# A new order for the first 430 entries of a hand-listed schedule, with new engines and PSUM pairs

## The chip, the cores and the metric

The kernel runs on one core of a Trainium2 chip. The metric is the device time of one execution in microseconds (us); lower is better. In this text PE is the matmul engine (TensorE), DVE, ACT and POOL are VectorE, ScalarE and GpSimd, and SP is the engine that issues the DMAs.

## The reference

A linear recurrence over 768 time steps (4 batches, 8 heads, head dimension 40), and behind it a two-layer MLP (320 to 2048 to 320) on its 3072 output rows, all in FP32:

```python
for t in range(S):
    y[:, :, t] = einsum('bhd,bhde->bhe', rt, state)
    Sa = einsum('bhde,bhe->bhd', state, at)
    state = state * wt[:, :, None, :] - einsum('bhd,bhe->bhde', Sa, bt) + einsum('bhd,bhe->bhde', vt, kt)
x = y.transpose(0, 2, 1, 3).reshape(B * S, H * D)
h = x @ w_in
out = (h / (1 + exp(-1.702 * h))) @ w_out
```

## The kernel before

Time is cut into 12 chunks of 64 steps, and the batches into two pairs: 24 units, numbered i = 2 x chunk + pair. Within a unit the recurrence is written as small matrices of one head and one chunk (64x64), four of which share the array as 64x64 quadrants. For each unit there are these steps, by the names of their PSUM tiles:

- `ps_cum` and `ps_cumc`: running sums of the logarithm of the decay, by time and by channel. ACT makes the factors FT, GT, wch (from `ps_cumc`) and G (from `ps_cum`) of them; products with FT and GT scale the inputs `ak` and `b` in place, products with G make `kh` and `bh`.
- `ps_A`, `ps_RV`, `ps_N`: scores. `ps_N` needs the scaled `ak` and `b` and begins the inversion of a triangular matrix; `ps_A` and `ps_RV` are masked by DVE into A and RV.
- `ps_level`: five rounds of that inversion. Each round is a matmul task (with an `ident` part in units 0 to 3), a copy of PSUM to PT or W, and a transposition into EX by DVE, on which the next round waits. Then `ps_Q` and `ps_T` finish the matrix T.
- `ps_B` (two halves), `ps_X`: the right side and the solution M; for chunks behind the first also `ps_zT` and `ps_rz`, which read the state.
- `ps_y`: the output and the new state. Units of one pair follow each other through the state, so unit 2 needs unit 0's `ps_y`, and unit 3 unit 1's.

The output of two units goes to memory and comes back turned as `xT_all`, and the chunk's MLP follows: `ps_up` (40 tasks a chunk, 64x256 matmuls), the gelu on ACT into g, and `ps_down`. The weights arrive as FP64 in eight pieces of four DMAs each (`w_sb`, `extra` and `xT_all` hold the raw pieces) and are turned into FP32 by ACT, DVE and POOL (L447 to L463).

Nothing sets the order but a list. Every step is a task with its possible engines, and `ORDER` names all 2700 tasks in the order in which they are issued: an entry is the task's number, a letter for the engine (p PE, a ACT, d DVE, g POOL, s SP) and, for tasks that use PSUM, which of four PSUM pairs they take. `Plan.listed` reads it:

```python
for one in text.split():
    e = next(e for e in ENGINES if ENGINES[e] in one)
    n, bank = one.split(ENGINES[e])
    t = self.tasks[int(n)]
    assert e in t.engines and t.after <= done and (e == "SP" or (t.pair is None) == (not bank))
    t.engine, t.bank = e, int(bank or 0)
```

and the kernel ends in `for t in plan.listed(ORDER): t.fn(t)`. Each engine works off its entries in the order of the list; between engines semaphores hold a task back until what it needs is there. All DMAs are issued by SP in one queue. Matmuls all stand in one helper, `mm`, which is line L300 of the profile.

Numbers that help to follow the list, for unit 0: 87 `ps_cum`, 88 `ps_cumc`, 89 and 90 the factors, 93 to 95 the products, 98 `ps_A`, 100 `ps_RV`, 103 `ps_N`, 107, 110, 113, 116 and 119 the five levels, 126 `ps_Q`, 128 `ps_T`, 130 and 132 `ps_B`, 134 `ps_X`, 136 `ps_y`. Unit 1: 142, 143 sums, 154 A, 156 RV, 159 N, 163 to 175 the levels, 190 X, 192 y. Unit 2: 264, 265 sums, 288 N, 292 to 304 the levels, 316 zT, 319 rz, 321 and 323 B. Unit 3: 334, 335 sums, 353 A, 355 RV, 358 N, 362 to 374 the levels, 386 zT, 389 rz. 198 to 207, 209 to 218 and so on are `ps_up`. DMAs of unit 0: 0 logw, 5 ak (two DMAs), 6 b (two), 7 rv (two), 8 RV, 9 time.

Of the kernel before, what the change touches and what calls it, by code (L numbers as in the profile page):

```python
# [119 lines left out]
214p1 389p2 66d 472a3 483g 204p0 390a2 560s 371p3 67d 306a 53s 215p1 71s 482s 216p1 372a3 217p1 476a 220p2 373d3 68g 218p1  # L120
221p2 477d 219a1 205p0 222p2 206p0 223p2 224p2 207p0 55a 311p3 225p2 79s 312d3 80s 226p2 208a0 58d 313p1 374p3 314d1 227p2 56d
379a3 228p2 229p2 57d 326p0 230a2 59g 393p1 327d0 378a3 391p2 394a1 375d3 231p0 558s 392d2 376a 232p0 233p0 395d1 559s 81s 73a
78s 234p0 480s 381p2 235p0 328p1 481s 382a2 74d 377a3 485d 380a3 236p0 75d 492a 242p2 486d 243p2 82a 76d 484d 77g 383p3 237p0
384d3 244p2 329d1 330d1 488p3 473d 238p0 531d 245p2 487g 246p2 489d3 85d 532p1 239p0 533a1 396p3 331d 332s 474s 475s 534a1
240p0 247p2 397d3 562s 241a0 535p1 83d 490p3 536a1 84d 398p0 572a 491d3 86g 550p1 555s 561s 253p3 399d0 551a 333s 400d0 254p3
401d 402s 554s 255p3 552a1 564d 493p0 705s 556a 567g 570p1 403s 494d0 248p2 563d 566g 249p2 495d0 498d 256p3 571d1 565g 250a2
496a0 251d2 252s 696p1 497g 557d 539p0 537p2 704s 257p3 538a2 540d0 258p3 553d 611d 697a 499d 573p2 784s 700s 259p3 576a2
574d2 710d 260p3 541d0 575d2 404p0 578d 261a3 577g 405p0 579d 698a1 568p2 711g 500p1 406p0 569d2 501a1 407p0 262d3 263s 708s
580p2 702a 502d1 408p0 582d2 409p0 503d 410p0 583d 504a 612p3 411p0 584g 613d3 412p0 614d3 413p0 505p1 709d 414a0 426p3 506d1
427p3 428p3 507d1 429p3 699d 581d2 430p3 615p1 785s 706s 701s 703d 431p3 616a1 585p0 432p3 508d 586a0 433p3 587d0 434p3 509a  # L130
588d 435p3 589d 448p2 436a3 510p1 590p0 511a1 449p2 592d0 591a0 512d1 415p3 513d 416p3 593d 514a 417p3 594g 418p3 515p0 419p3
# [4 lines left out]
623d0 780s 776a 549s 756d 730p3 624p0 456d2 457d2 731d3 458s 459p2 777a1 778g 732d3 786s 788g 781a 779s 626d0 460p2 625d0 627g
733d 795p1 835d 734a 461p2 735p3 791g 462p2 628s 736a3 796d1 737d3 716p0 792g 738d 463p2 782d 739g 1011s 920p1 757p3 925s
464p2 717d0 758a3 629s 759a3 790d 465p2 740p0 789d 466p2 741a0 742d0 921a 797p3 467d2 760p0 1008s 468d2 800a3 923d 652p2 469s
761d0 922a1 653p2 926a 930s 798d3 714p1 799d3 654p2 924s 802d 801g 655p2 934d 803a 656p2 836p0 657p2 715d1 658p2 659p2 837d0
762p3 838d0 927d 660p2 763a3 661p2 764p1 662a2 743d 630p0 744d 928s 631p0 632p0 765d1 804p3 766d1 633p0 805a3 806d3 634p0 807d  # L140
635p0 808a 745p2 636p0 748d2 637p0 749d2 839p1 933g 750d2 638p0 840a1 1009s 751d2 639p0 809p3 746d2 935g 640a0 641p1 810d3
642p1 793p2 747a 811d3 674p0 812d 794d2 813a 752p3 643p1 753a3 814p2 644p1 815a2 816d2 754p3 645p1 755d3 646p1 817d 647p1 818a
767p2 841p3 768d2 648p1 842a3 649p1 819p2 650p1 820a2 821d2 675p0 769p3 822d 651a1 823d 771d3 931s 770d3 772g 824p2 936d 676p0
827a2 828a2 942p1 829a2 677p0 1153s 830a2 937d 945a1 773s 663p3 825d2 664p3 943d1 1156s 826a 665p3 944d1 999p2 947d 946g 666p3
1000a 1004s 980d 940p1 948g 667p3 941d1 668p3 774s 669p3 670p3 831p1 671p3 1001a2 1002d 1003s 832d1 672p3 1005a 1013d 678p0
673a3 1006d 833p2 843p1 679p0 834d2 1007s 844d1 938p2 845d1 680p0 939d2 846p3 681p0 847d3 949p1 1012g 682d0 848p2 950a1 683d0
1014d 684s 685p3 849d2 1015g 1010s 850d2 1021p0 1016g 951d1 686p3 1024a0 1232s 851d 1235s 981p2 687p3 982a2 952d 852s 1022d0
983a2 953g 1144p1 1023d0 688p3 1026d 1145a 1149s 1025d 1027g 984p2 1059d 689p3 1154s 954p0 853s 985a2 1147g 690p3 1158d 1148s
955a0 956d0 986p2 1146a1 957d 1150a 691p3 958d 987a2 1151d 988p0 692p3 989a0 1152s 990d0 959p1 693a3 865p2 960a1 694d3 866p2
961d1 867p2 695s 962d 868p2 963d 1028p0 869p2 1029a0 1030d0 870p2 1031d 1157g 871p2 1159d 1032a 1060p3 872p2 873p2 1061a3  # L150
874p2 1062d3 1033p1 875a2 854p0 1035d1 855p0 1036d 856p0 1037d 1063p3 857p0 1064d3 1034a1 858p0 964p2 859p0 965a2 966d2 1038p1
967d 860p0 1039a1 1040d1 861p0 1041d 1017p3 968a 1042g 862p0 1018d3 863p0 969p2 864a0 876p1 970d2 877p1 972d2 971g 1043p3
973d2 878p1 1044a3 974d2 879p1 975d2 880p1 881p1 1045d3 1019p0 1046d 976p2 1047a 882p1 1020d0 1233s 883p1 977a2 1166p3 884p1
1169a3 1167d3 1377s 978p0 885p1 1168d3 898p2 1171d 1170g 886a1 979d0 887p3 1172a 1048p0 991p1 1051a0 888p3 1052a0 992d1 889p3
1053a0 890p3 1054a0 891p3 1049d0 993p1 1050a 1067p0 994d1 1160g 1155s 892p3 1161d 1068a0 893p3 894p3 1069d0 1380s 895p3 1204d
1065p0 995d1 896p3 996d 1066a0 1231s 1055p1 899p2 897a3 1056d1 997s 1173p0 1223p3 900p2 1174a0 1175d0 1228s 1176d 1224a 1177g
1057p1 901p2 1058d1 1070p0 998s 1164p1 1225a3 1226d 1236g 1227s 1071d0 902p2 1229a 1165d1 1162p3 903p2 1238d 1163d3 904p2
1237d 1178p0 1230d 905p2 1179a0 1180d0 1245p1 906a2 1181d 1072p3 1248a1 1456s 907d2 1182g 1246d1 908s 1247d1 909p0 1250d 1234s
1239g 1073d3 1251a 910p0 1240g 1074d3 1249d 1183p2 1459s 1283d 1368p1 911p0 1184a2 1075d 1373s 912p0 1185d2 1369a 1076s 1186d
# [978 lines left out]
```

## Time and profile before

| | |
|---|---|
| device time, three runs | 678.22, 678.64, 679.32 us (median 678.64) |
| span of the profiled execution | 676.5 us; no separate time is given for it, so the runs' median stands beside it, 2.1 us above |
| PE busy | 648.5 us, 96% of the span |
| DVE, ACT, POOL busy | 444.6, 331.6, 175.3 us |
| DMA | 69.74 MB, mean 103 GB/s |

The profile counts times from the first instruction. In the views, "<-" behind an idle time names what ended it; "issue" is a wait with no semaphore that the profile shows. A matmul of the program stands as two in the trace (FP32 takes two passes), so 16 matmuls of a task are "x32". The granted clock is 1.00 at full speed and 0.50 at half.

### The profile page before, as it was taken

What the parts mean: (1) busy time and instruction counts of PE and PEld (TensorE: products, weight loads), DVE (VectorE), ACT (ScalarE), POOL (GpSimd) and SP (SyncE); (2) the same over time, 40 slices, a digit from 0 to 9 for tenths busy, and PEclk for the clock granted to TensorE, in tenths of its full rate; (3) what the DMA queues carried; (4) which work ended last, traced back from release to release, by engine and by line L of the source; (5) the groups of instructions that cost most, each with busy time, mean ns of one, the idle gap of its engine ahead of it and who ended that gap; (6) DMA issues with size and microseconds to landing.
All of it is one profiled execution on the core that took longest, in us unless ns stands there. A gap on an engine that the chain in (4) does not pass through costs nothing.

```text
span 676.5 us, 42217 instructions
## 1 busy us (share of the span) xinstructions
PE 648.5 (96%) x19488; PEld 553.4 (82%) x19488; DVE 444.6 (66%) x908; ACT 331.6 (49%) x710; POOL 175.3 (26%) x204
## 2 busy tenths in 40 slices
PE   5768999999999999999999999999999999999997
PEld 5657887987998987788888888798888798798785
DVE  4786787777867667767776587768656766675001
ACT  4676755534564655664545445455454354252110
POOL 6344244224123123123123211322412421300000
PEclk9899999999999999999999999999999999999999
DMA  7983736315314314432404413513412411200200
GB/s 230 300 289 94 232 107 187 103 43 154 108 47 149 93 58 117 121 108 72 118 22 132 141 34 109 156 33 108 140 39 71 122 53 54 61 14 15 61 12 20
DMA packets 35313, 69.74 MB, mean 103 GB/s; under 512 B 5440, under 2 KB 14656, under 8 KB 35136
## 3 DMA queue, kind: packets, MB, share of 16 engines
q1 hardware_dynamic: 35136, 67.03, 32.6%
q8 instruction: 153, 2.51, 1.5%
q14 instruction: 24, 0.20, 0.1%
HBM read 59.15 MB, written 7.86 MB: 99 GB/s over the span
## 4 chain that ended last, share of the span: by engine, by line
PE 93%; DMA 2%; DVE 2%; issue 1%; ACT 1%; DVEq 0%; SPq 0%; ACTq 0%
PE ps_up L300 31%; PE ps_down L300 30%; PE ps_level L300 9%; PE ps_y L300 5%; PE ps_B L300 5%; PE ps_X L300 2%; PE ps_N L300 2%; PE ps_rz L300 2%; PE ps_RV L300 2%; PE ps_A L300 2%; PE ps_zT L300 1%; DMA ak<-in_ak 1%; PE ps_cum L300 1%; PE ps_T L300 1%; DMA b<-in_b 1%
## 5 line engine op out<-in xcount | busy, mean ns | idle before, releaser
L300 PE MATMUL ps_up<-xT_all,w_sb 64*64 64x256 f32 x3840 | 251.0, 377 | 0.8 <-issue 0.4
L300 PE MATMUL ps_down<-w_sb,g 64*64 64x320 f32 x3072 | 237.0, 430 | 0.2 <-ACT zr L877 0.2
L300 PEld LDWEIGHTS ps_up<-xT_all,w_sb 64*64 64x64 f32 x3840 | 170.1, 133 | 15.9 <-issue 1.5
L300 PEld LDWEIGHTS ps_down<-w_sb,g 64*64 64x64 f32 x3072 | 128.0, 133 | 42.8 <-ACT zr L877 0.4
L996 ACT ACTIVATE g<-ps_up 128x1024 f32<-128x1024 f32 x48 | 49.2, 1024 | 45.4 <-PE ps_up L300 45.0
L715 POOL TENSOR_TENSOR EX<-ES,quads 128x512 f32<-128x512 f32 x29 | 38.3, 1322 | 112.7 <-DVE ES L708 74.9
L300 PEld LDWEIGHTS ps_level<-W,EX 64*64 64x64 f32 x2560 | 57.8, 134 | 6.7 <-DVE T L838 0.5
L758 ACT COPY W<-ps_level 128x512 f32<-128x512 f32 (+1 forms) x56 | 29.5, 527 | 67.7 <-PE ps_level L300 65.7
L760 DVE TENSOR_TENSOR E<-two,ps_level 128x256 f32<-128x256 f32 x80 | 33.1, 415 | 34.2 <-ACT W L758 30.1
L300 PE MATMUL ps_level<-W,EX 64*64 64x64 f32 (+1 forms) x2560 | 55.4, 217 | 0.1
L713 ACT ACTIVATE EX<-ES,quads 128x256 f32<-128x256 f32 x80 | 36.3, 501 | 31.0 <-DVE ES L708 30.3
L619 POOL TENSOR_TENSOR ak<-ak,FT 128x512 f32<-128x512 f32 x16 | 20.9, 1305 | 76.6 <-DMA ak<-in_ak 53.4
L708 DVE STREAM_TRANSPOSE ES<-E 128x256 f32<-128x256 f32 x80 | 35.3, 443 | 4.4
L300 PE MATMUL ps_level<-PT,EX 64*64 64x64 f32 (+2 forms) x1280 | 32.8, 235 | 5.1 <-DVE EX L729 3.7
L300 PEld LDWEIGHTS ps_level<-PT,EX 64*64 64x64 f32 x1280 | 30.8, 139 | 8.3 <-DVE EX L729 4.2
L300 PE MATMUL ps_y<-M,bh 64*64 64x104 f32 (+1 forms) x768 | 35.6, 250 | 0.7 <-DVE M L915 0.4
L300 PE MATMUL ps_y<-RV,kh 64*64 64x104 f32 (+1 forms) x768 | 35.6, 251 | 0.0
L899 ACT COPY B<-ps_B 128x416 f32<-128x416 f32 (+1 forms) x34 | 16.6, 492 | 33.4 <-PE ps_B L300 33.2
L300 PEld LDWEIGHTS ps_y<-RV,kh 64*64 64x64 f32 x768 | 28.3, 137 | 2.6 <-DVE M L915 0.5
L689 DVE COPY_PREDICATED PT<-within,ps_N 128x256 f32<-128x256 uint32 x40 | 17.8, 444 | 18.5 <-ACT P L697 13.5
L915 DVE TENSOR_TENSOR M<-ps_X,later 128x832 f32<-128x832 f32 (+1 forms) x24 | 23.8, 993 | 8.3 <-PE ps_X L300 8.1
L300 PE MATMUL ps_B<-RV,A 64*64 64x104 f32 (+1 forms) x768 | 27.9, 252 | 1.1 <-issue 1.1
(131 smaller groups left out, 1088.2 us busy)
## 6 DMA issues: line engine op xcount, KB each, us to landing
ak<-in_ak SPq DMA_DIRECT2D x48, 160.0 KB
rv<-in_rv SPq DMA_DIRECT2D x48, 160.0 KB
time<-in_time SPq DMA_DIRECT2D x24, 320.0 KB
xT_all<-x_dram SPq DMA_DIRECT2D x48, 160.0 KB
wc<-in_wc SPq DMA_DIRECT2D x20, 264.0 KB
logw<-in_w SPq DMA_DIRECT2D x24, 160.0 KB
...
```

Of the source, the lines that this page charges most:

```text
L300: nc.tensor.matmul(o, lhsT, rhs, start=start, stop=True, skip_group_check=True)
L619: plan.add(R, {"DVE": 690.0, "POOL": 1270.0, "sbuf": True}, lambda t: of(t.engine).tensor_mul(ahT(), ahT(), FT_of(i)), reads=T("ak", "FT") ...
L689: plan.add(R, dve(256), lambda t, n=n: nc.vector.copy_predicated(tiles_of(at(E0_t, i)), every(within_of(n), [128, 2, 4, 32]), blocks(psum( ...
L708: plan.add(rank, dve(256), lambda t: nc.vector.transpose(ES(n), source(t)), writes=[key("ES", n, 6)], **reads)
L713: nc.scalar.activation(dst[:, :, h], ES(n), ACT.Copy, scale=quads[:, h, :1])
L715: of(t.engine).tensor_mul(dst, ES(n).unsqueeze(2).to_broadcast([128, 8, 2, 32]), quads.unsqueeze(1).to_broadcast([128, 8, 2, 32]))
L758: plan.add(rank, any2(512 - 8 * past), lambda t: copy(t.engine)(tiles_of(W(n + 1))[:, :, :, past:], blocks(psum(t, ""), 64)[:, :, :, past: ...
L760: plan.add(rank, dve(256), lambda t: nc.vector.tensor_sub(tiles_of(E(n + 1)), every(two32, [128, 2, 4, 32]), blocks(psum(t, ""), 64)[:, :, ...
L899: plan.add(R, any2(4 * wide), lambda t: copy(t.engine)(dst(), some(psum(t, "")[:, :, :208])), writes=[("Bv", i)] if x and c > 0 else T("B" ...
L915: plan.add(R + 1, dve(8 * wide), lambda t: nc.vector.tensor_tensor(M_of(i)[:, :, :wide].rearrange("p (j b) n -> p b j n", b=2), some(psum( ...
L996: plan.add(-45, {"ACT": 1030.0, "table": "gelu"}, lambda t: nc.scalar.activation(g_of(c * NQ + q).rearrange("p m r n -> p r m n"), psum(t, ...
```

## The change

The list alone is changed. Its first 430 entries hold the same 430 tasks as before in a new order, of which 26 run on another engine, and with other PSUM pairs. From entry 430 on the tasks, their order and their engines are the same; the numbers of the four PSUM pairs are renamed there. The first 430 entries are the start of the kernel: the loads and the conversion of the weights, units 0 to 3, the first steps of units 4 and 5, and the MLP of the first chunk up to a part of its `ps_down`.

The diff, cut to the entries up to the first `ps_up` (209p1 before, 198p3 after), and one pair of lines from the part behind:

```
-0s 5s 7s 8s 9s 3a 6s 87p0 88p1 24s 89a1 1s 2s 12s 102a 95d 100p2 90a0 93d 158a 101d2 98p3 96g 10s 94d 17s 97g 16s 99d3 103p1
-4a 11s 132p0 104a1 105d1 142p2 26s 143p3 133a0 106d 130p1 14s 144a3 13s 107p0 15s 18s 151g 108a0 109d0 51s 131a1 110p3 27s
-149g 150d 111a3 112d3 159p0 156p1 145a2 161d0 160a0 152g 113p3 345s 92a 162d 25s 153d 114a3 163p2 42s 115d3 34s 19a 274s 264p0
-165d2 265p3 164a2 22d 266a3 166p2 20d 273s 21d 33s 43s 167a2 154p3 168d2 23g 35s 28a 157d1 116p2 155d3 169p1 117a2 118d2 267a0
-279d 63s 280g 119p3 277s 171d1 36s 44s 120d3 343s 125d3 278g 124d3 29d 126p2 170a1 123a3 30d 172p1 122a3 127a2 121a 31d 128p2
-54s 173a1 287a 288p0 289a0 129d2 32g 174d1 134p3 147s 37a 290d0 175p2 135d3 180a2 146s 178a2 275s 176d2 136p1 179a2 479s 38d
-181a2 45s 39d 177a 282g 291d 91s 138a1 182p0 188p3 281d 183a0 186p2 139d 137a1 283p0 187a2 184p1 189a3 40d 276s 292p2 46a
-284d0 41g 285p3 185d1 344s 148a 286d3 190p0 293a2 294d2 334p1 335p3 357a 140s 191d0 268g 336a3 315d 192p2 47d 337a1 348d 316p0
-194a2 295p3 349d 61s 317a0 195g 60s 347s 358p1 296a3 62s 297d3 360d1 318a0 298p3 271a 361d 319p0 338g 300d3 196s 193a2 320a0
-346s 355p2 385d 270s 48d 299a3 362p0 356d2 351g 301p3 363a0 364d0 350g 269s 141s 386p2 197s 302d3 365p0 387a2 352g 359a1 303d3
-388a2 323p1 367d0 366a0 321p3 49d 324a1 304p2 322a3 478s 325d1 50g 353p0 309a2 470p3 354d0 209p1 307a2 210p1 310a2 305d2 211p1
...
+158a 0s 3a 88p0 87p3 9s 102a 5s 6s 89a0 90a3 93d 94d 103p0 1s 95d 4a 7s 96d 143p2 105d0 97g 104d0 142p3 8s 14s 106d
+107p1 144a2 145a3 18s 108a1 45s 100p0 98p3 101d0 152g 99d3 109d1 130p3 110p0 11s 10s 149g 111a0 150d 153g 2s 159p2 44s
+131d3 132p3 133a3 43s 42s 161d2 160a2 112d0 113p1 162d 163p2 92a 115d1 46a 114a1 49d 151g 116p1 164a2 117a1 165d2 118d1
+166p0 167d0 265p2 264p3 119p1 266a2 268g 168d0 169p0 344s 120d1 125d1 126p2 16s 287a 47d 170a0 267a3 171d0 172p0 15s
+154p3 273s 48d 24s 127a2 124d1 174d0 122a1 123a1 128p1 173a0 175p2 270s 155d3 12s 25s 27s 13s 17s 121a 36s 181a2 129d1
+156p1 179a2 134p3 278g 135d3 274s 19a 22d 26s 180a2 28a 279d 136p3 20d 176d2 178a2 50g 157d1 186p1 138a3 137d3 29d 91s
+177a 148a 288p2 290d2 277s 182p0 291d 188p3 187a1 139d 280g 281d 275s 292p1 289d2 189a3 282g 334p2 285p3 183a0 21d 184p0
+357a 293a1 276s 294d1 286d3 185d0 35s 335p1 343s 23g 190p0 140s 315d 191d0 347s 295p3 297d3 336a1 192p0 296a3 348g 338g
+33s 337a2 350d 316p3 318a3 349d 317d3 298p2 352g 358p1 193a0 141s 319p3 30d 300d2 194a0 147s 320d3 146s 346s 360d1 361d
+359a1 283p0 299a2 271a 195g 345s 301p2 31d 362p1 303d2 34s 364d1 302a2 196s 284d0 363a1 355p2 37a 356d2 272d 365p1 367d1
+63s 197s 321p0 38d 60s 351g 470p3 62s 304p2 61s 366a1 368p1 32g 471a 40d 340s 472a3 369a1 322a0 305d2 307d2 71s 39d
+198p3 199p3 200p3 201p3 41g 385d 64a 310d2 202p3 203p3 204p3 205p3 206p3 309d2 308d2 370d1 311p1 306a 323p2 312d1 207p3
...
-524d0 440p1 525d0 441p1 442p1 526d0 527p3 718p0 929s 528a3 443p1 719d0 787s 444p1 720d0 529p3 445p1 721d0 446p1 530d3 600p0
+425a2 437p3 521d1 438p3 523d1 522g 439p3 524d1 440p3 525d1 441p3 442p3 526d1 527p2 718p1 929s 528a2 443p3 719d1 787s
...
```

More of the change, by code (lines that the diff above doesn't have):

```diff
@@ L120 @@
[L120 to L131, printed above, removed]
@@ L136 @@
[L136 to L147, printed above, removed]
@@ L148 @@
[L148 to L159, printed above, removed]
@@ new lines @@
+1764p1 1930d2 1864g 1956p0 1765p1 1931d2 1957a0 1766p1 1932d 1958a0 1767p1 1933d 1865p3 1768p1 1868a3 1934p2 1869a3
+1769p1 1935d2 1770p1 1870a3 1794p0 1871a3 1936d2 1937d 1771a1 1866d3 1772p2 1938d 1867g 1959p3 1773p2 1960a3 2129s
+1939p1 1774p2 1940a1 1941d1 1775p2 1942d 1872p3 1776p2 1943d 1873a3 1777p2 2062p1 1778p2 2065a1 2063d1 2273s 1874p3
+1779p2 1875d3 1780p2 2064d1 1781p2 2067d 1887p3 1782a2 2066d 2068g 1783p1 1888d3 1784p1 1961p2 1944p3 1962a2 1785p1
+1945d3 1889p2 1947d3 1946a 1948d3 1949d3 1786p1 2051s 1950d3 1787p1 1891d2 1963p3 1890d2 1892g 1788p1 2127s 1964d3
@@ new lines @@
+2267g 2278d 2106p3 1810p2 2271d 2107a3 2268s 2108p1 1811p2 2109a1 2272s 2110d1 2148p0 1812p2 2149a0 2150d0 2151d 2180p3
+1813a2 2137p1 2181d3 2152a 1974p0 1814d2 1975p0 2138d1 1976p0 2182a3 1815s 2277g 1977p0 2279d 1978p0 1979p0 1980p0
+2183p2 1981p0 2184a2 2351s 1982p0 1983p0 2153p3 1984a0 1985p1 2154d3 1986p1 1987p1 2155d3 2079p2 2156d 1988p1 2157d
+2080a2 1989p1 2081d2 2018p3 2082d 2083a 2158p0 1990p1 2160d0 1991p1 2161d 2084p2 2159d0 2162a 1992p1 1993p1 2085d2
+1994p1 2086d2 2163p0 1995a1 2087d 1996p2 2164d0 2088g 1997p2 1998p2 2165d0 1999p2 2166d 2000p2 2167a 2089p1 2001p2
@@ new lines @@
+2092a1 2090d1 2002p2 2091d 2093a1 2003p2 2004p2 2094a1 2005p2 2095a1 2019p3 2006a2 2007p0 2008p0 2096p1 2286p2 2097a1
+2009p0 2287d2 2491s 2010p0 2288d2 2098p1 2011p0 2289d2 2290g 2012p0 2099d1 2168p2 2291d 2111p1 2292d 2171a2 2013p0
+2172a2 2112d1 2014p0 2173a2 2015p0 2174a2 2016p0 2169d2 2185p1 2170d 2017a0 2187p2 2186d1 2175p0 2020p3 2188a2 2349s
+2176d0 2189d2 2113p1 2021p3 2114d1 2280g 2275s 2324d 2177p0 2281g 2022p3 2178d0 2115d1 2190p2 2494s 2116d 2343p0 2023p3
+2191d2 2344a 2117s 2325p1 2024p3 2326d1 2327d1 2192p2 2345a0 2346d 2354g 2355d 2347a 2025p3 2118s 2356g 2352s 2328p1
@@ new lines @@
+2360d1 2210p3 2405p2 2211p3 2406d2 2566s 2212p3 2375p1 2213p3 2376a1 2377d1 2214p3 2378d 2215p3 2379a 2308p0 2216p3
+2310d0 2309a0 2217p3 2311d 2218p3 2312d 2380p2 2219a3 2220p1 2381d2 2221p1 2222p1 2382d2 2313p0 2383d 2223p1 2384a
+2314d0 2224p1 2316d0 2315g 2225p1 2317d0 2385p3 2318d0 2226p1 2386a3 2319d0 2227p1 2228p1 2387d3 2320p2 2388d 2504p0
+2389d 2321a2 2229p1 2242p3 2507a0 2505d0 2230a1 2506d0 2509d 2508g 2231p2 2510a 2322p0 2390p1 2323d0 2232p2 2393d1
+2335p0 2394d1 2233p2 2395d1 2234p2 2396d1 2235p2 2336d0 2236p2 2237p2 2391d1 2407p0 2392a 2337p1 2408d0 2409p0 2339d1
@@ new lines @@
+2517a0 2262d1 2420p3 2586d2 2421p3 2263s 2422p3 2518d0 2617p1 2519d 2423p3 2618a1 2587d2 2520g 2424p3 2619a1 2588d
+2425p3 2589a 2620p0 2426p3 2621d0 2521p2 2427p3 2522a2 2523d2 2428p3 2524d 2429p3 2525d 2590p1 2430a3 2431p0 2591d1
+2432p0 2433p0 2592d1 2526p2 2593d 2434p0 2594d 2527a2 2435p0 2528d2 2436p0 2529d 2437p0 2530a 2595p1 2438p0 2596d1
+2439p0 2440p0 2597d1 2531p3 2598d 2441a0 2442p2 2599d 2443p2 2532d3 2444p2 2534d3 2533a 2600p1 2535d3 2445p2 2446p2
+2536d3 2601a1 2447p2 2537d3 2448p2 2602d1 2538p0 2603d 2449p2 2604d 2539a0 2450p2 2451p2 2540p3 2605p1 2452a2 2541d3
@@ L245 @@
+2656p2 2657p2 2658p2 2659p2 2660p2 2661p2 2662p2 2663p2 2664p2 2665p2 2680p1 2666a2 2667p3 2668p3 2669p3 2670p3 2671p3
+2672p3 2673p3 2674p3 2675p3 2676p3 2681p1 2677a3 2682p1 2683p1 2684p1 2685p1 2689p0 2686d1 2687d1 2690p0 2688s 2691p0
+2692p0 2693p0 2694p0 2695p0 2696p0 2697d0 2698d0 2699s
 """
```

192 lines of the change are left out of this document (103 added, 89 removed).

## The prediction

> **What bounds the kernel now.** I read the page first: its busy shares, the slices and the chain that ended last.
>
> ```profile
> span 676.5 us, 42217 instructions
> PE 648.5 (96%) x19488; PEld 553.4 (82%) x19488; DVE 444.6 (66%) x908; ACT 331.6 (49%) x710; POOL 175.3 (26%) x204
> ...
> PE   5768999999999999999999999999999999999997
> ...
> q8 instruction: 153, 2.51, 1.5%
> ...
> PE 93%; DMA 2%; DVE 2%; issue 1%; ACT 1%; DVEq 0%; SPq 0%; ACTq 0%
> ```
>
> TensorE is the bound, and only the first four slices (17 us each) are not full. So an order of the first 430 entries can win only there. The windows view, PE alone, says how much (columns: stretch, its length, PE busy, granted clock, DMA share, GB/s):
>
> ```profile
> 16.10:19.60 3.50, 1.79 (x67) 0.99 0.99 341
> 19.60:23.00 3.40, 3.40 (x105) 0.50 0.80 293
> ...
> 36.70:40.10 3.40, 1.88 (x86) 1.00 0.93 265
> ...
> 46.90:50.30 3.40, 1.27 (x50) 1.00 0.99 357
> 50.30:53.70 3.40, 3.40 (x87) 0.50 0.06 20
> ...
> 67.50:80.00 12.50, 11.28 (x274) 1.00 0.69 216
> 80.00:108.50 28.50, 28.50 (x830) 1.00 0.50 160
> 108.50:660.00 551.50, 550.83 (x16535) 1.00 0.29 85
> ```
>
> From 80 us on PE is never idle; the PE tasks of the first 430 entries, counted along the trace, end at about 108.5 us, well inside that full part, and behind it only 0.67 us of idle is left in 551.5. Hence the rule of my sum: the same 123 PE tasks lie in the first 430 entries of both orders, so the change is worth what it does to PE's idle time and half-clock time before it is full, and everything behind moves along. The waits view over the first 108.5 us says what PE waited for:
>
> ```profile
> PE ps_level L300 <- DVE EX L729: 3.7, 3, 1.7
> PE ps_cum L300 <- POOL logw L367: 3.7, 1, 3.7
> PE ps_RV L300 <- DMA rv<-in_rv: 2.2, 2, 1.6
> PE ps_cum L300 <- issue: 2.1, 1, 2.1
> ...
> PE ps_rz L300 <- issue: 0.8, 1, 0.8
> ...
> PE ps_up L300 <- issue: 0.4, 1, 0.4
> ```
>
> Two kinds stand here: the latency of two units' inversions (level, PSUM copy, transposition, next level), and "issue". The latter are waits inside a task, with no semaphore. The q8 line gives their meaning: 153 packets carry 2.51 MB, 16.4 KB each, a page of PE's instructions; a page not yet there stops PE. The largest, 2.1 us, ends at 50.2, in the stretch 46.90:50.30 with the DMA engines 0.99 busy, and behind it the clock is at half for 3.4 us, which costs 1.7.
>
> **The change part by part.** Only the list ORDER changes; no instruction is added or removed. From entry 430 on tasks and engines are the same, and the PSUM pair numbers are renamed one to one (0 to 1, 1 to 3, 3 to 2, 2 to 0): nothing. In the first 430, 26 tasks change their engine: 15 go from ACT to DVE, 2 back, 5 from DVE to POOL, 4 back.
>
> ```profile
> L619 POOL TENSOR_TENSOR ak<-ak,FT 128x512 f32<-128x512 f32 x16 | 20.9, 1305 | 76.6 <-DMA ak<-in_ak 53.4
> ```
>
> A product that goes to POOL takes 1.3 us where DVE takes 0.72 (row below at 7.29). I count it at nothing, since POOL is 26% busy and the products of units 1 and 3 stand over a microsecond ahead of the scores that read them; without that cover it is 0.6 us each. The 83 DMA entries keep their number and are reordered on SP's one queue; what that does to b is counted next, and a later weight piece only moves ps_up, which the walk holds. I walk the new list: an instruction starts when its engine is free and its last input is there, with the durations of rows.
>
> *Start to unit 0's ps_N.*
>
> ```profile
> 4.24 1.12 PE L300 MATMUL ps_cumc<-edges,logw 64*64 64x65 f32 x32
> ...
> 5.44 0.66 ACT L565 ACTIVATE FT<-ps_cumc 128x256 f32<-128x256 f32 x2 [1.91 <-PE ps_cumc L300]
> 5.98 0.67 ACT L565 ACTIVATE GT<-ps_cumc 128x256 f32<-128x256 f32 x2
> ...
> 7.29 0.72 DVE L619 TENSOR_TENSOR ak<-ak,FT 128x512 f32<-128x512 f32 x1
> ...
> 10.25 0.78 DVE L621 SCALAR_TENSOR_TENSOR b<-b,GT 128x512 f32<-128x512 f32 x1 [0.29 <-DMA b<-in_b]
> ...
> 11.29 1.14 PE L300 MATMUL ps_N<-b,ak 40*64 40x64 f32 x32 [1.30 <-DVE b L621]
> ```
>
> b (2 DMAs of 80 KB) stands behind 1280 KB (logw, ak, rv, RV, time by the sizes of the page's DMA list), and 1440 KB have landed by 10.2. In the new order rv and RV (480 KB) come later: 960 KB, in proportion from the first issue at 0.8, 0.8 + 9.4 x 2/3 = 7.1, an estimate. ps_cumc goes ahead of ps_cum (3.68 to 4.24), so GT ends at 6.65 - 0.56 = 6.1, the ak product at 6.8, the b product at 7.1 + 0.78 = 7.9. ps_N starts at 7.9 in place of 11.29: 3.4 earlier. The RV score that stood ahead of it goes behind level 0; the 2.2 us wait for rv goes with it.
>
> *ps_N to unit 0's ps_X.*
>
> ```profile
> 14.95 1.43 PE L300 MATMUL ps_level<-PT,EX 64*64 64x96 f32 x32
> ...
> 16.71 0.80 ACT L792 COPY PT<-ps_level 128x768 f32<-128x768 f32 x1 [0.66 <-ACT wch L569]
> ...
> 17.55 0.72 DVE L729 STREAM_TRANSPOSE EX<-ps_level 128x512 f32<-128x512 f32 x1 [2.90 <-ACT PT L792]
> ...
> 29.19 0.89 PE L300 MATMUL ps_level<-PT,EX 64*64 64x96 f32 x32 [0.76 <-DVE EX L729]
> ...
> 31.55 0.67 PE L300 MATMUL ps_level<-PT,EX 64*64 64x32 f32 x32
> ```
>
> One level costs 1.43 at the half clock of the start and 0.89 later (same 32 matmuls); with its ident part (0.4), copy and transposition a round is 2.8 to 3.4 us, if nobody is in the way. In the list of before ACT's and DVE's weight conversions and unit 1's work stood between rounds: the fourth level starts at 29.19, the fifth at 31.55. Walked in the new list the rounds start at 11.0, 16.0, 20.2, 23.1 and 26.5: 5 us earlier at the end. Then unit 1's levels are interleaved, and ps_X of unit 0 starts at 34.5 in place of 37.91.
>
> *ps_X to the first ps_up.*
>
> ```profile
> 35.90 0.85 PE L300 MATMUL ps_N<-b,ak 40*64 40x64 f32 x32
> ...
> 37.91 0.83 PE L300 MATMUL ps_X<-B,T 64*64 64x104 f32 x25 [1.17 <-DVE T L838]
> ...
> 61.75 0.54 PE L300 MATMUL ps_zT<-ident,zr 40*40 40x40 f32 x32
> ...
> 63.34 0.59 PE L300 MATMUL ps_B<-RV,A 64*64 64x104 f32 x16
> ...
> 64.10 0.53 PE L300 MATMUL ps_B<-RV,A 64*64 64x104 f32 x15
> ...
> 66.81 0.66 PE L300 MATMUL ps_A<-ak 40*64 40x64 f32 x32
> 67.28 0.47 PE L300 MATMUL ps_cum<-logw,edges 64*64 64x160 f32 x8
> 67.55 0.62 PE L300 MATMUL ps_up<-xT_all,w_sb 64*64 64x256 f32 x8
> ```
>
> Here the new list gives back. Unit 2's ps_N, ahead of ps_X in before (35.90), now stands behind unit 0's ps_y, which waits for M: it starts at about 40.1. Units 2 and 3 then have their five rounds each, and the first ps_up comes at 66.1 in place of 67.55. That holds one more page wait and one half-clock stretch near 57 us, as the old one did near 50. So 1.45 earlier. But by then the new list has left three tasks for later: ps_zT of unit 3 (0.5), one ps_B (63.34 to 64.10: 0.76), ps_A (0.47), together 1.75 (zT and A by their rows up to the next task), and has done one level of unit 3 that came after it before (0.89, about 1.05 with its ident part). Net 0.7 more to do.
>
> *First ps_up to full.* From here PE has work in plenty; 12.50 - 11.28 = 1.22 us of idle are left in 67.5:80, nearly all page waits (ps_rz 0.8, ps_up 0.4). The new list puts nine ps_up tasks in a row first, then seven between single others; a ps_up matmul is long, so a page of 256 instructions lasts longer there. I take 0.2 of the 1.22 as left: bounds are 0 and, if pages come late again, 1.22 or a little more.
>
> Sum: -1.45 + 0.7 - 1.0 = **-1.75 us** against the span of 676.5. The span lies 2.1 under the median of the runs, 678.64; that rest is not touched. Forecast 678.64 - 1.75, **676.9**.
>
> The clock is the least certain size. By the rows, a stretch of 3.4 us with 1.27 or 1.79 us of PE work was followed by half clock, one with 1.88 was not; a full one ended it. [...]
>
> **The rivals.** *Pages cost as much as before.* If the page waits behind the first ps_up stay at 1.2, the sum is -1.45 + 0.7 = -0.75: 677.9, not to be told from no change, since 0.2% (1.36 us) is what a measurement of this kernel can tell. For it: the new list loads the same weights, in the same crowded DMA engines. [...]
>
> *Half clock twice more: slower.* In the new list PE waits long for the copies and transpositions of units 2 and 3, at about 42 and 55 us. It decides when PE works under about 1.8 of 3.4 us in two windows beyond the one I count. Price: 1.7 each, 3.4 - 1.75 = +1.65: 680.3. DVE helps this rival: it takes 15 tasks of ACT, and is the fuller one already:
>
> ```profile
> 20.00:40.00 20.00, 14.31 (x551) 12.34 (x545) 16.98 (x27) 14.43 (x36) 8.91 (x5) 0.93 0.91 298
> ```
>
> DVE is busy 16.98 of 20 there, ACT 14.43; three or four moved tasks of 0.5 to 0.8 us would fill it.
>
> *The start's gain is kept.* If units 2 and 3 lose nothing after ps_X, and no half clock falls behind 23 us, the 3.4 us at ps_X stay, less 0.7, and with 1.0 of pages: -3.7, 674.9.
>
> **How the numbers follow.** Forecast 0.44; start's gain kept 0.16; no difference 0.18; slower 0.22. Faster by over 0.2% is the first two, 0.60. The range 674.0 to 680.3 reaches from a little under the third rival to the second, and leaves out 2 in 10 with longer chains of clock and page at either end.
>
> **What would show it.** Right: ps_N at 7 to 9 us, the fifth level near 26.5, ps_X near 34.5, the first ps_up at 65 to 67, "issue" waits under 0.5 us in total between there and 80, at most one half-clock stretch after 23 us. Wrong: ps_N still at 11 (b lands late whatever stands ahead), ps_up behind 68, two or more half-clock stretches after 23, DVE as the releaser of most PE waits between 20 and 60, or PE idle behind 110 us, where I count nothing.

## The result

The new kernel took 681.72 us (median of 20 runs, 678.26 to 685.17), the old one in the same comparison 678.40 (20 runs, 674.41 to 680.75): ratio 1.0059 with an interval of 1.0044 to 1.0073, so 3 to 5 us **slower**, where 1.75 us faster was forecast. (The ratio is taken over all executions, so it is not quite that of the two medians, which lie 3.3 us apart.) The profiled execution of the new kernel took 680.51 us with a span of 678.6, that of the old one had a span of 676.5.

The page after, the same lines as before (`mm` is line L307 in the new kernel, and the numbers of other lines move with it):

```profile
span 678.6 us, 42209 instructions
PE 648.0 (95%) x19488; PEld 539.1 (79%) x19488; DVE 452.1 (67%) x925; ACT 325.9 (48%) x689; POOL 178.4 (26%) x208
...
PE   5766999999999999999999999999999999999997
...
PE 92%; DVE 4%; issue 1%; ACT 1%; DMA 1%; SPq 0%; ACTq 0%; DVEq 0%
```

TensorE has the same work, and the loss is again within the first four slices: 5766 where 5768 stood; DVE is 4% of the chain that ended last, where it was 2%. The timeline of PE alone, with the forecast's milestones (start, length, operation, and in brackets the idle time ahead and what ended it):

```profile
7.86 1.16 PE L307 MATMUL ps_N<-b,ak 40*64 40x64 f32 x29 [2.38 <-ACT logw L533]
...
26.75 0.65 PE L307 MATMUL ps_level<-PT,EX 64*64 64x32 f32 x31
...
29.61 0.46 PE L307 MATMUL ps_Q<-ES,P 64*64 64x64 f32 x15 [0.48 <-issue]
...
35.50 0.33 PE L307 MATMUL ps_level<-PT,EX 64*64 64x32 f32 x5 [1.38 <-issue]
...
36.93 0.38 PE L307 MATMUL ps_X<-B,T 64*64 64x104 f32 x1
...
42.07 0.41 PE L307 MATMUL ps_y<-RV,kh 64*64 64x104 f32 x8 [0.91 <-issue]
43.29 0.65 PE L307 MATMUL ps_N<-b,ak 40*64 40x64 f32 x32
...
52.34 0.30 PE L307 MATMUL ps_X<-B,T 64*64 64x104 f32 x2 [1.42 <-issue]
...
59.74 0.56 PE L307 MATMUL ps_A<-ak 40*64 40x64 f32 x20 [1.33 <-issue]
...
69.67 0.64 PE L307 MATMUL ps_up<-xT_all,w_sb 64*64 64x256 f32 x5 [0.30 <-ACT G L598]
```

The first two milestones came as walked (7.9 and 26.5 forecast). From there the list ran late: unit 0's ps_X at 36.93 (34.5), unit 2's ps_N at 43.29 (40.1), the first ps_up at 69.67 (66.1; 67.55 before). The windows view shows one half-clock stretch behind 23 us, at 35.60, and PE nearly full from the first ps_up on (columns: stretch, its length, then PE, weight loads, DVE, ACT and POOL busy with their counts, granted clock, DMA share, GB/s):

```profile
35.60:39.00 3.40, 3.06 (x80) 2.74 (x79) 0.23 (x1) 2.42 (x7) 0.40 (x1) 0.51 1.00 320
...
67.50:80.00 12.50, 11.92 (x335) 11.11 (x332) 9.32 (x21) 8.41 (x16) 6.23 (x3) 1.00 0.60 208
80.00:108.50 28.50, 28.05 (x831) 24.60 (x826) 24.00 (x37) 19.33 (x36) 11.68 (x5) 1.00 0.65 201
108.50:660.00 551.50, 550.60 (x16533) 456.08 (x16529) 368.80 (x784) 261.67 (x544) 129.65 (x142) 1.00 0.29 85
```

The waits view of PE between 20 and 80 us, the new kernel first and then the old one (its largest rows; us in total, times, longest):

```profile
PE ps_level L307 <- DVE EX L736: 4.4, 5, 1.5
PE ps_level L307 <- ACT PT L799: 2.7, 4, 1.1
PE ps_y L307 <- DVE M L922: 1.4, 2, 1.2
PE ps_X L307 <- issue: 1.4, 1, 1.4
PE ps_level L307 <- issue: 1.4, 1, 1.4
```

```profile
PE ps_cum L300 <- issue: 2.1, 1, 2.1
PE ps_level L300 <- DVE EX L729: 2.0, 2, 1.2
PE ps_X L300 <- DVE T L838: 1.2, 1, 1.2
...
PE ps_level L300 <- ACT PT L792: 0.7, 1, 0.7
```

Summed over the whole view, waits for pages ("issue") are 5.8 us in both. Waits for another engine are 10.8 in the new kernel and 7.7 in the old.

How much is lost by the end of the changed entries can be read at one place. Ahead of this ps_N both orders have done the same 2784 passes of PE, counted by tile; the old kernel first, then the new one:

```profile
108.25 0.68 PE L300 MATMUL ps_N<-b,ak 40*64 40x64 f32 x32
```

```profile
111.04 0.69 PE L307 MATMUL ps_N<-b,ak 40*64 40x64 f32 x32 [0.34 <-issue]
```

The new order is 2.8 us late there. At the last pass of PE it is 2.0 late. So the whole loss of this pair arises within the changed entries.

### The profile page after: what moved, and what is told of

The parts are those of the page before. It is cut to its first block, busy times and chain, and to the rows that moved or that the text cites. A ratio compares the mean times of both kernels' runs of the same rounds, so it can differ in the third digit from the quotient of the medians.

```text
span 678.6 us, 42209 instructions
## 1 busy us (share of the span) xinstructions
PE 648.0 (95%) x19488; PEld 539.1 (79%) x19488; DVE 452.1 (67%) x925; ACT 325.9 (48%) x689; POOL 178.4 (26%) x208
## 3 DMA queue, kind: packets, MB, share of 16 engines
q8 instruction: 153, 2.51, 1.5%
HBM read 59.15 MB, written 7.86 MB: 99 GB/s over the span
## 4 chain that ended last, share of the span: by engine, by line
PE 92%; DVE 4%; issue 1%; ACT 1%; DMA 1%; SPq 0%; ACTq 0%; DVEq 0%
PE ps_up L307 31%; PE ps_down L307 30%; PE ps_level L307 9%; PE ps_y L307 5%; PE ps_B L307 5%; PE ps_X L307 3%; PE ps_N L307 2%; PE ps_RV L307 2%; PE ps_A L307 2%; PE ps_rz L307 1%; PE ps_zT L307 1%; DVE EX L736 1%; PE ps_T L307 1%; PE ps_Q L307 1%; PE ps_cum L307 1%
## 5 line engine op out<-in xcount | busy, mean ns | idle before, releaser
L307 PE MATMUL ps_up<-xT_all,w_sb 64*64 64x256 f32 x3840 | 246.1, 377 | 0.6 <-ACT G L598 0.3
L307 PE MATMUL ps_down<-w_sb,g 64*64 64x320 f32 x3072 | 238.5, 430 | 0.2 <-ACT zr L884 0.2
L307 PEld LDWEIGHTS ps_up<-xT_all,w_sb 64*64 64x64 f32 x3840 | 162.0, 133 | 21.4 <-DVE B L909 0.7
L307 PEld LDWEIGHTS ps_down<-w_sb,g 64*64 64x64 f32 x3072 | 125.8, 133 | 45.5 <-issue 0.4
L307 PEld LDWEIGHTS ps_level<-W,EX 64*64 64x64 f32 x2560 | 55.6, 134 | 8.2 <-DVE T L845 0.4
L307 PE MATMUL ps_level<-W,EX 64*64 64x64 f32 (+1 forms) x2560 | 53.9, 217 | 0.0
L307 PE MATMUL ps_level<-PT,EX 64*64 64x64 f32 (+2 forms) x1280 | 32.4, 236 | 9.1 <-DVE EX L736 5.0
L307 PEld LDWEIGHTS ps_level<-PT,EX 64*64 64x64 f32 x1280 | 29.9, 138 | 13.6 <-DVE EX L736 4.2
L307 PE MATMUL ps_y<-RV,kh 64*64 64x104 f32 (+1 forms) x768 | 34.7, 248 | 2.7 <-DVE M L922 1.4
L307 PE MATMUL ps_y<-M,bh 64*64 64x104 f32 (+1 forms) x768 | 34.5, 247 | 0.0
L307 PEld LDWEIGHTS ps_y<-RV,kh 64*64 64x64 f32 x768 | 26.7, 133 | 6.5 <-DVE M L922 2.5
L968 POOL TENSOR_TENSOR x<-zr,FT 128x128 f32<-128x128 f32 x44 | 22.2, 534 | 29.7 <-DVE zr L958 16.2
```

The lines of the kernel that those rows point to most:

```text
L307: nc.tensor.matmul(o, lhsT, rhs, start=start, stop=True, skip_group_check=True)
L968: of(t.engine).tensor_mul(x[:, b ^ u, b], both(i)[:, at, :64], FT_of(i)[:, at])
```

## The experiments

Four explanations were to be told apart: the order itself (PE waits longer for DVE and ACT), the 26 moved engines, the order of the DMAs, and the luck of where PE's page boundaries and half-clock stretches fall. On the chips of the experiments the old kernel took up to 3 us longer, so each ratio is to the old kernel on the same chip and in the same series; 0.001 is 0.7 us.

**Engines.** e1 and e2 exchange the engine letters alone, for example:

```
e1 (new order):  ... 104d0 -> 104a0, 131d3 -> 131a3, 153g -> 153d, 378d0 -> 378a0 ... (26)
e2 (old order):  ... 104a1 -> 104d1, 131a1 -> 131d1, 153d -> 153g, 378a3 -> 378d3 ... (26)
```

> The new order with the 26 tasks back on their old engines. Theory order (the order itself leaves PE without work, above all because ps_N of unit 2 stands behind unit 0's ps_y): stays 2.5 to 4 us above the kernel before, 681 to 682. Theory engines (products moved to POOL hold up DVE, 15 tasks fill DVE): loses at least half of the 3.3 us, 680 or less, and the 1.59 us of bounded at 28.7 and the 1.87 us of zr at 49.9 are gone. Theory pages and clock (the waits for PE's instruction pages and the half-clock stretches fall in other places): anything from -2 to +2 us against the new kernel, and the sum of issue waits before the first ps_up differs from 5.8 by as much.

> The old order with the 26 tasks on their new engines. Theory order: as before, within 0.7 us of 678.4. Theory engines: 1.5 to 3.5 us slower, 680 to 682. Theory pages and clock: within 2 us of before on either side, by whatever the issue waits and half-clock stretches become.

e1: 1.0095 (1.0058 to 1.0131), some 2.5 us worse than the new kernel, with intervals that overlap. e2: 0.9995 (0.9979 to 1.0012). So the engines cost the old order nothing, and giving them back does not help the new one. That is against the theory of the engines, but e1 (whose profiled execution, 693 us, was the slowest of its eight) reached the first ps_up at 67.2 and lost behind it, so the list was cut there:

```
e9:  the 13 tasks of entries 18 to 247 on their old engines
e10: the 13 tasks of entries 257 to 424 on their old engines
```

> The new kernel with the old engines for the 13 moved tasks that stand ahead of the first ps_up (entries 18 to 247); the 13 behind it keep their new engines. In e1 (all 26 back) the first ps_up came at 67.2 where the new kernel has 69.7, but 3.0 us of waiting for the mask A at 95 and 4.0 at 118 came behind it. Theory DVE queue (the tasks moved to DVE ahead of ps_up make DVE's one queue the chain between 42 and 50, where it is 9.45 of 10 us busy): ratio 0.999 to 1.003, first ps_up at 66.5 to 68, DVE under 9 in 40 to 50. Theory order: ratio stays 1.005 to 1.007. Theory DMA order: the same.

> The other half: old engines for the 13 moved tasks behind the first ps_up, new ones ahead. Theory DVE queue: the loss ahead of ps_up stays (first ps_up 69 to 70) and the waits of e1 at 95 and 118 come on top: ratio 1.008 to 1.013. Theory order: ratio 1.005 to 1.007.

e9: 1.0055 (1.0030 to 1.0080), no different from the new kernel, although unit 1's ps_y came at 49.6 in place of 53.9. e10: 1.0156 (1.0107 to 1.0205). PE's waits in e10 between 70 and 125 us:

```profile
PE ps_B L298 <- DVE A L636: 3.0, 1, 3.0
PE ps_B L298 <- issue: 1.9, 1, 1.9
PE ps_N L298 <- issue: 1.6, 1, 1.6
PE ps_rz L298 <- ACT zT L864: 1.0, 1, 1.0
```

The moves behind the first ps_up are needed in the new order: without them alone it is 6.6 us slower (1.0156 against 1.0059), and with the old engines ahead of ps_up too 2.7 us (e1 against e9). Those ahead of it cost neither order anything that shows (e9, e2). So the moved engines are not the loss. The theory of the DVE queue is not settled by e9, which left DVE as full between 40 and 50 us as it was. The windows rows of the new kernel and of e9 (DVE is the third engine):

```profile
40.00:50.00 10.00, 6.40 (x274) 5.34 (x271) 9.45 (x21) 5.62 (x14) 2.44 (x2) 1.00 0.50 155
```

```profile
40.00:50.00 10.00, 6.67 (x300) 5.99 (x304) 9.41 (x17) 6.79 (x23) 5.25 (x4) 1.00 0.69 195
```

The first ps_up of e9 came at 68.27, but in the fastest of its twelve executions. e11 below brought DVE down to 8.80 there.

**The start alone.** e8 puts the first 23 entries of the new list before the rest of the old one, on the old engines for the rest:

```
-0s 5s 7s 8s 9s 3a 6s 87p0 88p1 24s 89a1 1s 2s 12s 102a 95d 100p2 90a0 93d 158a 101d2 98p3 96g ... 103p1
+158a 0s 3a 88p1 87p0 9s 102a 5s 6s 89a1 90a0 93d 94d 103p1 1s 95d 4a 7s 96d 143p3 105d1 97g 104d1 8s 24s 2s ...
```

> The old order with the first 23 entries of the new one (time, ak and b of unit 0 ahead of rv; ps_cumc ahead of ps_cum; ps_N of unit 0 at once, at 7.9), everything behind in the old order. Theory start kept (the 3.4 us earlier ps_N is worth something in itself): 1 to 3 us faster, ratio 0.996 to 0.999. Theory other work (PE did other tasks in that time in the old order, so nothing is won): ratio 1.000 within 0.002. Theory pages and clock: as the second, but within 0.005.

1.0025 (1.0001 to 1.0048). PE's waits of e8 in the first 60 us:

```profile
PE ps_level L298 <- DVE EX L727: 5.0, 6, 1.6
...
PE ps_y L298 <- issue: 3.2, 1, 3.2
PE ps_N L298 <- DVE b L619: 3.0, 1, 3.0
```

ps_N starts at 8.5, 2.8 earlier than in the old kernel, and nothing is won. In the old order PE did the scores of unit 0 in that time. Longer waits for pages do not hide a gain: between 20 and 80 us they are 5.8 us, as in the old kernel.

**Pages.** I read "issue" as a wait for a page of PE's instructions. Two things in the traces speak for it: in the old and the new kernel every such wait of PE between 20 and 80 us (eight and six) stands 193 or 194 instructions behind a multiple of 256, in the order of PE's instructions, and it ends 1.2 to 1.6 us behind the end of a packet of queue q8, of which the profile of either kernel lists 153, with 2.51 MB. Filler matmuls that nothing reads are to shift these boundaries and to change nothing else.

```
e3, e4: +  for n in range(32): mm(warm[:64, n % 2, :64], full[:64, :64], full[:64, 64:], True)
e5, e6: +  for n in range(8):
        +      for b, u in QUARTERS: mm(fill[HALF[u], b, :64], full[HALF[b], :64], full[HALF[b], :64], True)
e13, e14: 16 of them at the start, 48 ahead of entry 432;   e15, e16: 48 and 16
```

> The new kernel with 32 matmuls more (64x64, on the constant full) in PE's idle 3.7 us at the start; nothing reads them. They shift every page boundary behind them by half a page (128 of 256 instructions) and do nothing else. Theory order or engines: 681.7 within 0.7. Theory pages and clock: over 1 us away from 681.7, more likely faster, since the old places (35.5, 42.1, 52.3, 59.7) are on the chain of units 0 to 2; 678.5 to 680.5.

> The kernel before with the same 32 matmuls at the start, every page boundary shifted by half a page. Theory order or engines: 678.4 within 0.7. Theory pages and clock: over 1 us away on either side, the 2.1 us wait at 50.2 and the half clock behind it gone or elsewhere.

e3 (new order) 1.0195 (1.0163 to 1.0227), e4 (old order) 1.0134 (1.0099 to 1.0170): a miss, since the filler itself took 7 us; the new order is 4.6 us behind here too. These are the rows of the filler in e3 and, for the next pair, in e5:

```profile
L307 PE MATMUL ps_fill<-full x64: 311/311/363, 1.4 to 8.2; 64*64 64x64 f32 x64
```

```profile
1.43 1.98 PE L307 MATMUL ps_fill<-full 64*64 64x64 f32 x64 [1.43 <-POOL full masks.py:199]
```

In one quadrant of the array the 64 passes come 107 ns apart, spread over four quadrants 27 ns. The pair with the filler spread:

> The new kernel with the 32 filler matmuls spread over the four quadrants of the array, so that they run side by side (about 27 ns apart, as ps_cumc's do: 1.7 us, done at about 3.2, before logw is there at 3.8). In e3 and e4 they stood in one quadrant, took 7.0 us and pushed ps_cumc from 3.8 to 8.1. Now only the page boundaries move by half a page, and PE is warm for 1.7 us more. Theory order: ratio to before as the new kernel's, 1.004 to 1.007. Theory pages and clock: outside 1.002 to 1.009, on either side.

> The kernel before with the same filler, side by side. Theory order: ratio 1.000 within 0.0015. Theory pages and clock: outside that on either side, by 1 us or more; the 2.1 us wait at 50.2 goes or falls elsewhere.

e5 (new) 1.0165 (1.0132 to 1.0197), e6 (old) 1.0117 (1.0093 to 1.0141). Half a page of shift costs the **old** kernel 7.7 us, more than the whole change; but the new order stays 2.4 us behind the old one with the same shift. Much of the 7.7 lies far behind the changed entries, where PE looks full. These are the windows rows of 140 to 660 us, the old kernel and then e6, whose execution is from a later series:

```profile
140.00:660.00 520.00, 519.54 (x15629) 441.50 (x15626) 341.43 (x734) 246.72 (x512) 118.18 (x129) 1.00 0.28 83
```

```profile
140.00:660.00 520.00, 517.82 (x15548) 448.94 (x15543) 342.62 (x737) 246.52 (x514) 118.37 (x129) 1.00 0.29 83
```

In the same 520 us e6 does 81 passes less, and PE is idle 1.7 us more. Set against the same pass of the old kernel, e6 is 2.1 us late at the 2800th (110.60 against 108.48) and 7.2 at the last (678.48 against 671.28), so 5.1 of it come behind the changed entries. e7 and e8, which ran on the same chip in the same series without a shift, lost 1.5 and 2.1 over these passes; some 3 us are then the shift's, by one execution each. So the next pairs add one whole page in total: the boundaries behind entry 431 stay where they are, and only those in the first 430 entries move.

> The new kernel with 64 filler matmuls, which nothing reads: 16 of them in PE's idle time at the start (0.9 us) and 48 behind entry 431 (about 1.4 us of PE time, on constants). Together they are one page of 256 instructions, so every page boundary behind entry 431 stands where it stood, and only those in the first 430 entries move, by a quarter page. Theory order (PE's waits for DVE and ACT in the new list): the new kernel stays 2.5 to 4 us above the old one with the same filler (e14), ratio of the two 1.004 to 1.006. Theory pages (the new list only has its boundaries in worse places): the difference to e14 changes by over 2 us from the 4.0 of the two kernels as they are, and its mean over the quarter shifts is near 0.

> The kernel before with the same 16 and 48. The filler behind entry 431 costs 1.4 us by itself, so 1.002 without any effect of the pages. Theory order: within 2 us of that. Theory pages: more than 2 us above it, since the old places would then be the lucky ones.

> The new kernel with 48 at the start (2.6 us, so ps_cumc starts some 0.3 later) and 16 behind entry 431 (0.5 us): boundaries of the first 430 entries moved by three quarters of a page, the rest in place. Theory order: 2.5 to 4 us above e16. Theory pages: a difference to e16 that has nothing to do with 4.0.

> The kernel before with the same 48 and 16. Without any effect of the pages 0.5 to 1 us above the kernel before, ratio 1.001. Theory order: within 2 us of that. Theory pages: more than 2 us above it.

e13 1.0102 (1.0068 to 1.0136) against e14 1.0049 (1.0026 to 1.0072); e15 1.0125 (1.0092 to 1.0157) against e16 1.0033 (1.0013 to 1.0053). At every place of the boundaries the new order is slower, by 2.4 to 6.6 us (table below). Single pairs are weak, since the new order has six executions in each: the intervals of e5 and e6, of e13 and e14 and of e17 and e18 below overlap. It is the same sign in all of them that counts. So the loss comes with the new list, not with the luck of its pages.

**Single edits of the new order.**

```
e7:  ... 156p1 179a2 134p3 278g [274s 279d] 135d3 19a 22d 26s 180a2 28a [288p0] 136p3 ...
e11: ... 286d3 185d0 [29d 21d] 35s ...      (29d was at entry 137, 21d at 159)
e12: 270s from entry 105 to behind 346s at 202
```

> The new kernel with three entries moved: b of unit 2 (274, keeping its place among the DMAs) and the product on it (279, DVE) ahead of unit 0's M (135), and ps_N of unit 2 (288) ahead of unit 0's ps_y (136). Theory order (ps_N of unit 2 standing behind ps_y costs the 2.9 us of waits between 40 and 52): ratio falls from 1.006 to 1.002 or less, ps_N of unit 2 at about 38.7, inside the 1.2 us that ps_y waits for M, and the 1.5 us wait of the first level of unit 2 shrinks. Theory pages and clock: the ratio moves by chance, and stays within 1.003 to 1.010.

> The new kernel with two steps of the weight conversion on DVE (29 and 21, 0.82 us each, at 43.75 and 47.53) moved behind unit 1's T (185). Theory DVE queue: ps_X and ps_y of unit 1, 49.99 and 53.85, come 0.7 to 1.5 us earlier, and the ratio falls by 0.001 to 0.002, to 1.004 to 1.005. Theory order or pages: 1.006, whatever ps_X does.

> The new kernel with one DMA (270, logw of unit 4, needed from 61 on) moved from entry 105 to behind entry 202, as late as in the old list. It waits for a buffer until 27.1 and holds SP's queue from 21.7 on; without it the eight DMAs behind it (rv and RV of unit 1, five weight pieces, b of unit 2) can be issued 4 to 5 us earlier. Theory DMA order: unit 1's and unit 2's steps and the page fetches at 35.5 to 42 find the queue free, ratio falls to 1.003 or less. Theory DVE queue: ratio 1.005 to 1.007.

e7: 1.0080 (1.0050 to 1.0109); unit 2's ps_N came at 38.45 (43.29), but PE waited 2.6 us for its b, which this list had let come late. e11: 1.0055 (1.0027 to 1.0083), with DVE busy 8.80 of the 10 us from 40 to 50 and unit 1's ps_y 0.9 earlier (52.92). e12: 1.0066 (1.0042 to 1.0089). None brings anything back that can be measured.

**The clock.** Three batches of filler keep PE busy through the waits of the start, in two whole pages:

```
e17 (old): 32 at the start, 48 behind 88 (ps_cumc), 32 ahead of 103 (ps_N), 16 ahead of entry 432
e18 (new): 32 at the start, 48 ahead of 103, 48 ahead of entry 432
```

> The kernel before with 128 filler matmuls that nothing reads, two pages of instructions in all, so that the boundaries behind entry 431 stand where they stood: 32 in PE's idle time at the start, 48 behind ps_cumc where PE waits for rv, 32 ahead of ps_N of unit 0 where it waits for b, 16 behind entry 431. PE is then busy without a break from 1.4 to 12. If the half clock of the start (until 16.1; 4.8 us of the kernel's time by the windows) is what these waits cost, the granted clock is full from about 6 to 9 on, the first level takes 0.9 in place of 1.4, and the kernel gains 1 to 3 us: ratio 0.996 to 0.999. If the waits for b, DVE and ACT set the pace there anyway, 1.000 to 1.003.

> The new kernel with the same number: 32 at the start, 48 ahead of ps_N of unit 0 (it waits 2.4 us there), 48 behind entry 431 (1.4 us of PE time). Half clock as the loss: the new kernel's 1.006 falls to 1.003 or less, although the filler behind costs 0.002. Waits as the loss: 1.006 to 1.010, with a full clock from 6 to 9 on and longer waits in its place.

e17: 1.0073 (1.0047 to 1.0099). e18: 1.0106 (1.0053 to 1.0160). The groups of PE between 5 and 16 us, by shape, the old kernel and then e17 (count, busy us, mean ns of one):

```profile
L300 PE MATMUL ps_level<-PT,EX 64*64 64x96 f32 x28 | 1.4, 362 | 0.0
...
L300 PE MATMUL ps_N<-b,ak 40*64 40x64 f32 x32 | 1.1, 317 | 1.3 <-DVE b L621 1.3
```

```profile
L300 PE MATMUL ps_N<-b,ak 40*64 40x64 f32 x32 | 1.0, 229 | 1.3 <-DVE b L628 1.0 <-issue 0.3
L300 PE MATMUL ps_level<-PT,EX 64*64 64x96 f32 x32 | 0.9, 248 | 0.3 <-ACT GT L572 0.3
```

The clock column has no record of the start: it reads 1.00 there in both. The durations tell it. In e15, where 0.50 is recorded from 7.5 to 24.5, this level takes 1.50 to 1.56, and 0.89 behind that. In the old kernel, where 0.50 is recorded from 19.6 to 23.0, 28 of a level's 32 passes take 1.36 from 21.37 on. So in e17 the clock is full, the first level takes 0.9 in place of 1.4, and the kernel is 5 us slower. Between 20 and 80 us page waits are 7.0 (5.8 in the old kernel), waits for engines 8.6 (7.7), the clock 0.89 (0.95). Of its 7.1 us at the last pass, 4.4 came behind the 2800th, where only the last batch of filler (about 0.5) and no wait of the start plays a part, and 2.7 before it. In e18 a pass of the levels between 5 and 20 us takes 305 ns in the mean, in the new kernel 366 and in e17 248, so there the clock was full for a part of that time. No gain from it shows in either order.

**The five pairs.** Each pair has the two orders with the same filler, on one chip. Waits are sums of the waits view, 20 to 80 us; clock is the granted one there; PE busy is of the 60 us from 80 to 140.

| pair | new, old (us) | difference | waits for engines | page waits | clock | PE busy 80:140 |
|---|---|---|---|---|---|---|
| as they are | 681.72, 678.40 | 3.3 | 10.8, 7.7 | 5.8, 5.8 | 0.97, 0.95 | 59.09, 59.79 |
| quarter (e13, e14) | 687.23, 682.92 | 4.3 | 10.5, 7.0 | 3.1, 7.5 | 0.89, 0.92 | 58.04, 59.10 |
| half (e5, e6) | 690.22, 687.87 | 2.4 | 12.0, 6.4 | 5.8, 11.2 | 0.91, 1.00 | 57.92, 59.65 |
| three quarters (e15, e16) | 688.71, 682.11 | 6.6 | 10.0, 7.6 | 5.1, 5.9 | 0.73, 0.89 | 59.20, 59.74 |
| warm start (e18, e17) | 688.91, 685.88 | 3.0 | 12.4, 8.6 | 2.7, 7.0 | 0.94, 0.89 | 57.51, 59.30 |
| mean difference | | 3.9 | +3.7 | -3.0 | -0.04 | -1.2 |

The waits for engines are longer in every pair. Page waits are shorter or the same, by 3.0 us on average. That a page lands while PE waits for something else, so that the two take each other's place, is my reading of this; it was not shown. The clock is lower in three pairs of five; 0.04 of 60 us is 2.5 us, most of it from one pair. With 1.2 us less of PE work behind 80 us the sum is 3.7 - 3.0 + 2.5 + 1.2 = 4.4. The terms come from the one profiled execution of each kernel, and the spans of these differ by 2.1, -0.8, 4.4, 8.1 and 3.7, on average 3.5: in the quarter pair the profiled execution of the new order was the faster one. So the sum is near the mean, but the terms of a single pair do not add up that well, and the split into terms is an argument from five pairs, not a proof.

Of the 3.7 us, 3.1 stand in one row of the view: ps_level waiting for PT from ACT, 2.7, 4.2, 4.2, 3.3 and 4.4 us in the new order, 0.6 to 0.7 in every profile of the old. The quarter-page pair, e13 and then e14:

```profile
PE ps_level L307 <- ACT PT L806: 4.2, 4, 2.3
```

```profile
PE ps_level L300 <- ACT PT L799: 0.7, 1, 0.7
```

The timeline of ACT in the new kernel, and in a fence of its own that of DVE, shows the longest of these waits:

```profile
57.21 0.59 ACT L960 COPY zr<-ps_y 128x512 f32<-128x512 f32 x1
60.01 0.63 ACT L704 ACTIVATE P<-ps_N,quads 128x128 f32<-128x128 f32 x2 [2.20 <-DVE PT L729]
60.52 0.80 ACT L799 COPY PT<-ps_level 128x768 f32<-128x768 f32 x1
```

```profile
58.67 0.64 DVE L884 COPY zr<-ps_rz 128x512 f32<-128x512 f32 x1
59.25 0.67 DVE L729 TENSOR_TENSOR PT<-ps_N,within 128x512 f32<-128x512 f32 x1
```

The copy of unit 2's third level (299, level done at 57.3) stands in ACT's queue behind a step of unit 3 (359, P), which waits until 60.0 for DVE, itself behind 30, 300 and 320; unit 2's fourth level starts at 61.38. The old list has 299 ahead of 359. Changing these two back was not tried. e9 says that it need not pay: there 299 started at 55.8, the waits for PT fell to 1.8 us, a page wait of 2.1 us stood at 57.3 in their place, and the time stayed (680.30 us in this execution, 680.51 in the new kernel's).

**What stays open:** which of the reordered entries would have to go back. No single edit did it, and no run here beats the old kernel, so none is put forward. The order of the DMAs was tried with one DMA alone (e12); no wait of PE for a DMA stands between 20 and 80 us in the ten executions of the table, so it could act only through the other engines or the pages. The new PSUM pairs were never tried by themselves. Waits in which the engine named writes nothing that the step reads, and so probably frees a pair, are 1.3 us in the new kernel (ps_cum for P, ps_RV for PT, ps_up for G) and 1.9 in the old, which speaks against them.

## Why the prediction was wrong, point by point

- *Start to ps_N* (7.9): right, 7.86. That it is worth 3.4 us was already doubted in the walk, which let it shrink to 1.45; e8 shows no gain from it.
- *ps_N to ps_X*: right up to the fifth level (26.5; 26.75), wrong behind it. ps_X came at 36.93, not 34.5: page waits of 0.48 and 1.38 us and the half clock from 35.60, of which I had counted none there. This is the larger part of the term that failed, told next.
- *ps_X to the first ps_up*: here stands the term that failed, the -1.45. The first ps_up was forecast at 66.1 and came at 69.67, so the -1.45 became +2.1 (69.67 - 67.55). The walk was 0.25 us too early at the fifth level, 2.4 at ps_X, 3.2 at unit 2's ps_N (40.1; 43.29) and 3.6 at ps_up. So 2.2 of the 3.6 us arose between the fifth level and ps_X, 0.8 up to unit 2's ps_N (a page wait of 0.91 in ps_y) and 0.4 behind it, where a half-clock stretch of 1.7 that I had near 57 did not come in this execution and waits stood in its place. **The step that failed is the walk itself:** I walked two chains of latencies with the durations of rows, took each engine as free when its turn came, and counted one page wait. The trace has six before ps_up, 5.8 us. The 67.55 it was compared with is measured, and holds 4.7 us of such waits. And PE waits 10.8 us for other engines where it had waited 7.7; the queue of ACT, with a step of another unit ahead, was in the list to be read.
- *First ps_up to full*: right. From 67.5 to 80 PE is idle 0.58 us (1.22 before), of which 0.01 falls behind the first ps_up, and no page wait is among it. One of 0.39 came later, at 87.70. From the first ps_up to the ps_N at 111.04 the new order loses 0.7 more, where +0.7 - 1.0 was forecast.
- *Behind 80 nothing*: wrong by 0.7 us in the profiled execution (59.09 busy of 60 against 59.79) and by 1.2 on average, about half of these 60 us being still changed entries. Behind the changed entries the rule that everything moves along is rough: the new order won 0.8 us back there, and e6 lost 5.1.
- *Engines at nothing*: right for the 13 ahead of ps_up (e9, e2), wrong for the 13 behind: the new order needs them, 6.6 us (e10), as a gain that the sum did not hold.
- *The rivals.* The one that forecast slower had the sign and 680.3, but not the mechanism of this execution: two more half-clock stretches did not come (0.97 of the clock against 0.95), waits did. Over the five pairs the clock is 0.04 lower, so half clock has a part in some executions. The border of about 1.8 us of work is not sharp: from 38.97 to 42.38 PE worked 1.61 and the clock stayed at 1.00 behind it. That DVE is the releaser of most PE waits between 20 and 60, named as a sign of being wrong, came true (6.9 of 8.2 us of waits for engines), but it is so in the old kernel too (4.8 of 7.7). *Pages cost as before* was right as a sum, 5.8 and 5.8 us between 20 and 80, in single waits of 0.3 to 2.1. The mean of the chances leaned on gains that were each real at their place and worth nothing in sum.
